# Three more clearing matmuls ahead of the first transposition

## The chip, the cores and the metric

The kernel runs on one core of a Trainium2 chip. The metric is the time of one execution on the device in microseconds (us); the median of three runs of the kernel before is 458.16 us (457.68 to 458.56). Profiles are of one execution each, and times inside them count from the first instruction.

## The reference, cut to what matters

Two layers are applied in turn, twice: a sliding-window attention (32 heads of 16, window 256) and a dense layer with a gelu, both behind a layer norm and with a residual. x is 2048 x 512 in bf16.

```python
x = A_x
x = x + _A_ref(_layernorm(x, axis=-1), A_wqkv, A_wo)
x = x + _B_ref(_layernorm(x, axis=-1), B_w1, B_b1, B_w2, B_b2)
x = x + _A_ref(_layernorm(x, axis=-1), A_wqkv, A_wo)
x = x + _B_ref(_layernorm(x, axis=-1), B_w1, B_b1, B_w2, B_b2)
```

The instructions that the change adds compute nothing of this. They multiply zeros by zeros and write zeros into PSUM, and every later user of PSUM starts its own sum.

## The kernel before, in words

The 2048 rows are cut into 16 tiles of 128 rows, and two tiles make an attention block. For each tile the layer norm takes the statistics on VectorE (bn_stats, L727; bn_aggr, L729; the epsilon, L731), the power of -1/2 on GpSimd (L734), and the normalised tile xn on VectorE (L737). TensorE then transposes xn in four matmuls of 128 columns against the identity (L36, called from tr, L757), and ScalarE or VectorE copies the result out of PSUM to xnTA (L713, L715). For each block, TensorE makes Q and K (groups of four matmuls with 256 columns, L32) and V (512 columns). ScalarE and VectorE move these out of PSUM (Q: L713 and L715; K: L824; V: L713). Then TensorE makes scores for 512 positions at a time and ScalarE takes their exponential (L903), a mask is multiplied in (L924), and E times V follows. Layers of the dense part run between these visits.

Nothing is scheduled while the program runs. Each piece of work is a node, added with `add`; a list ORDER, written out by hand, says in which order the nodes are put on their engines, TURNS which engine takes a node that has a choice, BANKS which PSUM bank it gets. `run` of the class `_List` walks that list and works out a start and an end of each node from stated durations. These times decide no order. They are used in one place, `spread`: an instruction of TensorE that would wait for several semaphores hands some of these waits to earlier matmuls that, by the planned times, start late enough. So a stated duration can move a wait from one matmul to another, and does nothing else.

The engine with the change is TensorE. Its program begins with two clear nodes (L665 to L677): VectorE sets a tile of zeros, and the two nodes multiply it by itself into PSUM banks 0 to 7, and then again into banks 0 to 4, 13 matmuls of 512 columns in all. They wait for the zeros alone. Behind them TensorE's queue holds four transpositions of tile 0, four of tile 1, 12 matmuls for Q and K of block 0, eight transpositions of tiles 2 and 3, 22 more matmuls for Q and K, and the first 16 matmuls of the scores. TensorE takes its queue in this order.

The loads go out on the queues of SyncE and ScalarE at the start: x in four pieces, and the three parts of the Q, K, V weights, then Wo, W1 and W2.

```python
for n, took in ((8, 3420.0), (5, 1300.0)):
    add("pe", clear(n), took, reads=["zero", "g0"], writes=["ps:init0", "ps:init1"], prio=-200, geo="f")
```

Of the kernel before, what the change touches and what calls it, by code (L numbers as in the profile page):

```python
# [185 lines left out]
class _List:  # L186
# [13 lines left out]
    def add(self, eng, fn, dur, reads=(), writes=(), prio=0.0, alloc=(), free=(), after=(), geo=None, table=None,  # L200
            issue=0.0, alt=(), war=(), lock=False, joins=()):

        i = len(self.nodes)
        deps = set(after)
        for r in tuple(reads) + tuple(joins):
            if r in self.lw:
                deps.add(self.lw[r])
        for w in tuple(writes) + tuple(war):
            if w in self.lw:
                deps.add(self.lw[w])  # L210
            deps.update(self.lr.get(w, ()))
        for r in reads:
            self.lr.setdefault(r, []).append(i)
        for w in writes:
            self.lw[w] = i
            self.lr[w] = []
        deps.discard(i)
        n = 0
        if eng == "pe":
            c = _Count()  # L220
            fn(c, _Anywhere())
            n = c.n
        self.nodes.append(dict(
            eng=eng, fn=fn, dur=dur, reads=list(reads), writes=list(writes), prio=prio, joins=tuple(joins),
            jdeps=frozenset(self.lw[r] for r in joins), alloc=alloc, free=tuple(free), deps=deps, geo=geo, table=table,
            issue=issue, lock=lock, alts=((eng, fn, dur),) + tuple(alt), n=n, behind=None,
            heavy=any(a[0] == "pool" and a[2] > 600.0 for a in ((eng, fn, dur),) + tuple(alt)),
        ))
        return i
# [69 lines left out]
def bass_interleave_layers__sliding_block__dense_activation_gelu__prompt_kernel(  # L299
# [72 lines left out]
    with ExitStack() as kctx:  # L372
# [294 lines left out]
        def clear(n):  # L667

            def fn(e, B):
                for b in range(n):  # L670
                    r = e.matmul(ps[:, b, :], gT[:, 0, 0:P], zero, start=True, stop=True)
                return r

            return fn

        for n, took in ((8, 3420.0), (5, 1300.0)):
            add("pe", clear(n), took, reads=["zero", "g0"], writes=["ps:init0", "ps:init1"], prio=-200, geo="f")  # L677

        def dma(fn, writes, reads=(), dur=2200.0, prio=0.0, issue=640.0, eng="sp"):
# [431 lines left out]
        for i in order:  # L1111
            nd = PL.nodes[i]
            n = 1
            if nd["eng"] == "pe":
                c = _Count()
                nd["fn"](c, B)
                n = c.n
# [32 lines left out]
```

## Time and profile before

| | |
|---|---|
| median of three runs | 458.16 us |
| lowest, highest | 457.68, 458.56 us |
| the profiled execution's own time | 460.18 us |
| its span, first to last instruction | 458.4 us |
| outside the span | 1.8 us |
| TensorE busy | 444.1 us, 97% |
| ScalarE busy | 389.7 us, 85% |
| VectorE busy | 368.5 us, 80% |
| mean granted clock of TensorE | 0.993 |

The profiled execution is 2.0 us longer than the median. A row of the timeline gives the start, the length, the engine, the line, the operation, what it writes and reads, how many instructions are merged in it, and in brackets how long the engine was idle before, and what ended that. A row of the windows gives a stretch, its length, for each engine the busy time and in brackets the number of instructions that touch it, the granted TensorE clock as a share of full speed, the DMA share and the rate. The clock's first record begins at 6.05 us; ahead of it the column prints 1.00 without a record.

### The profile page before, as it was taken

The numbers are of one execution on the slowest core, as the hardware profiler recorded it, in microseconds if no ns is written. First come the engines' busy times: TensorE is split into PE (matmuls) and PEld (weight loads), VectorE is DVE, ScalarE is ACT, GpSimd is POOL, SyncE is SP. The second block draws the span as 40 slices with busy tenths as digits, with TensorE's granted clock in tenths as the row PEclk, the third lists the DMA queues.
The fourth block names the chain that finished last, engine by engine and source line by source line (L and its number), as shares of the span: only waits on it lengthen the run. The fifth ranks groups of instructions, "written<-read, shape, count | busy, mean of one in ns | idle before, by whom it ended". The sixth has DMA issues, their size and how long they took to land.

```text
span 458.4 us, 19422 instructions
## 1 busy us (share of the span) xinstructions
PE 444.1 (97%) x8790; PEld 238.7 (52%) x8790; DVE 368.5 (80%) x749; ACT 389.7 (85%) x462; POOL 234.7 (51%) x266
## 2 busy tenths in 40 slices
PE   7999999989899999999999999999999999999997
PEld 3655655645453554645455545546464554545664
DVE  5899988999777888989889888899788888677411
ACT  2899999999789999899997999889987999792442
POOL 5377666565768266332565467754355243462400
PEclk9999999999989999999999999999999999999999
DMA  8910000001110020100120000201012002201211
GB/s 271 370 62 4 4 3 3 4 3 26 40 35 1 9 44 9 43 3 11 21 68 3 5 23 15 60 9 24 3 23 58 3 11 52 72 2 33 67 52 36
DMA packets 27839, 18.17 MB, mean 40 GB/s; under 512 B 15852, under 2 KB 27244, under 8 KB 27756
## 3 DMA queue, kind: packets, MB, share of 16 engines
q1 hardware_dynamic: 26172, 15.35, 12.8%
q8 instruction: 69, 1.13, 1.1%
q10 hardware_dynamic: 1584, 1.57, 1.0%
q14 instruction: 14, 0.11, 0.1%
HBM read 11.41 MB, written 5.51 MB: 37 GB/s over the span
## 4 chain that ended last, share of the span: by engine, by line
PE 75%; ACT 21%; DVE 1%; DMA 1%; issue 1%
PE ps L32 74%; ACT E L903 16%; ACT gT L1069 2%; ACT gT L1061 1%; PE ps L36 1%; ACT L903 1%; ACT L1061 1%; DMA X<-in_A_x_dram 1%; DVE stat L727 0%; DVE X L784 0%; DVE xn L737 0%; ACT xnTA L715 0%; DVE statmv L729 0%; DVE veps L731 0%
## 5 line engine op out<-in xcount | busy, mean ns | idle before, releaser
L903 ACT ACTIVATE E<-ps 128x1024 bf16<-128x1024 f32 x304 | 286.3, 1048 | 24.9 <-PE ps L32 24.1
L924 POOL TENSOR_TENSOR E<-E,mask 128x512 bf16<-128x512 bf16 (+1 forms) x133 | 140.3, 1070 | 91.8 <-DVE E L924 46.9
L32 PE MATMUL ps<-W_sb,gT 128*128 128x512 bf16 x448 | 120.1, 380 | 0.0
L32 PE MATMUL ps<-xnTB,W_sb 128*128 128x512 bf16 (+1 forms) x560 | 113.1, 337 | 0.0
L32 PE MATMUL ps<-xnTA,Wqkv_sb 128*128 128x256 bf16 x512 | 76.3, 279 | 1.2 <-ACT xnTA L715 0.7
L32 PEld LDWEIGHTS ps<-xnTB,W_sb 128*128 128x128 bf16 x560 | 51.6, 98 | 43.4 <-ACT E L903 3.9
L784 DVE TENSOR_TENSOR X<-X,ps 128x512 bf16<-128x512 bf16 x64 | 43.3, 681 | 33.9 <-PE ps L32 33.0
L1069 ACT ACTIVATE gT<-ps,b1T 128x512 bf16<-128x512 f32 (+1 forms) x92 | 48.5, 588 | 23.9 <-PE ps L32 23.4
L32 PE MATMUL ps<-QT,KT 32*64 32x320 bf16 (+4 forms) x2976 | 65.7, 259 | 2.9 <-ACT E L903 1.2
L734 POOL TENSOR_TENSOR rstd<-veps,mhalf 128x1 f32<-128x1 f32 x64 | 36.2, 572 | 52.2 <-DVE veps L731 50.4
L32 PEld LDWEIGHTS ps<-W_sb,gT 128*128 128x128 bf16 x448 | 39.6, 98 | 42.2 <-issue 8.4
L32 PEld LDWEIGHTS ps<-xnTA,Wqkv_sb 128*128 128x128 bf16 x512 | 47.2, 100 | 23.9 <-issue 3.1
L32 PEld LDWEIGHTS ps<-QT,KT 32*64 32x64 bf16 x2976 | 27.6, 103 | 51.1 <-ACT E L903 32.3
L924 DVE TENSOR_TENSOR E<-E,mask 128x512 bf16<-128x512 bf16 (+1 forms) x129 | 51.1, 424 | 2.5 <-ACT E L903 2.5
L32 PE MATMUL ps<-E,Va 64*17 64x128 bf16 (+3 forms) x3872 | 49.3, 230 | 3.5 <-issue 1.7
L1033 POOL TENSOR_TENSOR X<-X,b2b 128x512 bf16<-128x512 bf16 x32 | 36.6, 1153 | 30.0 <-DVE TM L994 12.4
L989 DVE STREAM_TRANSPOSE TT<-ps 128x1024 f32<-128x1024 f32 x32 | 39.9, 1248 | 13.8 <-PE ps L32 13.1
L32 PEld LDWEIGHTS ps<-E,Va 64*17 64x17 bf16 x3872 | 39.5, 85 | 19.1 <-PE ps L32 6.3
L727 DVE BATCH_NORM_STATS2 stat<-X 128x6 f32<-128x512 bf16 x64 | 43.0, 678 | 3.9 <-DMA X<-in_A_x_dram 3.4
L824 DVE TENSOR_TENSOR KT<-ps,parmask 128x1024 bf16<-128x1024 f32 x32 | 38.6, 1206 | 1.3 <-PE ps L32 1.2
L1058 DVE TENSOR_SCALAR gT<-ps,b1T 128x512 bf16<-128x512 f32 (+1 forms) x48 | 31.8, 672 | 6.9 <-PE ps L32 6.3
L32 PE MATMUL ps<-Wqkv_sb,xnTA 128*128 128x512 bf16 x128 | 36.8, 381 | 0.5 <-issue 0.5
(49 smaller groups left out, 330.0 us busy)
## 6 DMA issues: line engine op xcount, KB each, us to landing
W_sb<-in_B_w_dram SPq DMA_DIRECT2D x2, 1792.0 KB, 17.5
scr_x<-xs_ SPq DMA_DIRECT2D x104, 32.0 KB, 1.6
xnTB<-scr_x SPq DMA_DIRECT2D x26, 128.0 KB, 2.8
out_dram<-X SPq DMA_DIRECT2D x16, 128.0 KB, 1.7
Wqkv_sb<-in_A_wqkv_dram ACTq DMA_DIRECT2D x3, 512.0 KB, 7.5
X<-in_A_x_dram SPq DMA_DIRECT2D x1, 1024.0 KB, 12.2
X<-in_A_x_dram SPq DMA_DIRECT2D x2, 256.0 KB, 4.6
X<-in_A_x_dram SPq DMA_DIRECT2D x1, 512.0 KB, 8.8
```

The lines of the kernel that those rows point to most:

```text
L32: return self.e.matmul(*a, **k)
L727: add("dve", lambda e, B: e.bn_stats(stat6[:, k6, :], X[:, t, :]), 590, reads=["X%d" % t], writes=["st%d" % k6], prio=prio)
L734: add("pool", lambda e, B: e.tensor_tensor(out=rstd[:, k : k + 1], in0=veps[:, k : k + 1], in1=mhalf[:], op=ALU.pow), 535, reads=["ve%d" % ...
L784: add("dve", lambda e, B: e.tensor_tensor(out=X[:, t, :], in0=X[:, t, :], in1=ps[:, B[g][0], :], op=ALU.add), d_psum(512), reads=["X%d" % ...
L824: add("dve", lambda e, B, g=g, i=i: e.tensor_tensor(out=KT[:, kb, :, 2 * i : 2 * i + 2, :].rearrange("p a c q -> p a (c q)"), in0=ps[:, B[ ...
L903: add("act", lambda e, B, g_=g_, gi=gi: e.activation(E[:, 2 * gi : 2 * gi + 2, e0 : e0 + 512], ps[:, B[g_][0] : B[g_][0] + 2, :], AF.Exp, ...
L924: op = lambda e, B, Ew=Ew, Mw=Mw: e.tensor_tensor(out=Ew, in0=Ew, in1=Mw, op=ALU.mult)
L989: add("dve", lambda e, B: e.transpose(TT[:, s].rearrange("p a c q d -> p a (c q d)"), ps[:, B[g][0] : B[g][0] + 2, :].rearrange("p a n -> ...
L1033: add("pool", lambda e, B: e.tensor_tensor(out=X[:, t, :], in0=X[:, t, :], in1=b2b[:], op=ALU.add), 1110, reads=["X%d" % t, "b2b"], writes ...
L1058: add("dve", lambda e, B, g=g, fc=fc: e.tensor_scalar(out=gT[:, fc, 0:M], in0=ps[:, B[g][0], 0:M], scalar1=b1T[:, fc : fc + 1], scalar2=No ...
L1061: add("act", lambda e, B, fcs=fcs: e.activation(gT[:, fcs[0] : fcs[-1] + 1, 0:M], gT[:, fcs[0] : fcs[-1] + 1, 0:M], AF.Gelu_apprx_tanh, sc ...
L1069: add("act", lambda e, B, g=g, fc=fc: e.activation(gT[:, fc, 0:M], ps[:, B[g][0], 0:M], AF.Gelu_apprx_tanh, bias=b1T[:, fc : fc + 1], scal ...
```

## The change

The second of the two clear nodes clears eight banks in place of five, so that there are 16 clearing matmuls in place of 13. Its stated duration goes from 1300 to 2000 ns.

```diff
-        for n, took in ((8, 3420.0), (5, 1300.0)):
+        for n, took in ((8, 3420.0), (8, 2000.0)):
             add("pe", clear(n), took, reads=["zero", "g0"], writes=["ps:init0", "ps:init1"], prio=-200, geo="f")
```

In the built programs the instructions of VectorE, ScalarE, GpSimd and SyncE and their waits are the same. On TensorE three matmuls are added behind the 13th, and two waits move: one for a DMA goes from a score matmul to the matmul with W1 right behind it, and one for ScalarE goes from the last of four transpositions to the score matmul right behind it.

## Prediction

> **What bounds the kernel now.** First the page's busy shares and its clock row, to see which engine is full and where its clock drops.
>
> ```profile
> PE 444.1 (97%) x8790; PEld 238.7 (52%) x8790; DVE 368.5 (80%) x749; ACT 389.7 (85%) x462; POOL 234.7 (51%) x266
> ...
> PEclk9999999999989999999999999999999999999999
> ```
>
> TensorE (PE) is busy 97% of the span. The clock row's slices are 11.5 us long and hide a short drop; the windows view below shows two. Next, the chain of waits, followed from the first transpositions on.
>
> ```profile
> 8.01 0.41 PE ps L36 x4
> 8.42 0.02 issue
> 8.44 0.61 ACT xnTA L715
> 9.04 0.05 issue
> 9.09 2.42 PE ps L32 x12
> 11.51 0.85 PE ps L36 x8
> 12.37 8.78 PE ps L32 x128
> 21.14 0.02 issue
> 21.16 27.61 ACT E L903 x30
> ```
>
> From 9.09 us PE work alone sets the pace up to 21.14; then ScalarE's exponentials follow one another for 27.61 us. What PE saves before 15 us brings the first exponential (15.51 us in ScalarE's timeline) forward, and all behind it. Ahead of 9.09 the chain is the load of x and the layer norm: the clears are not on it. Third, the windows view: PE's busy time in stretches of 3.41 us, and its granted clock.
>
> ```profile
> 6.05:9.47 3.42, 1.71 (x15) 1.00 1.09 349
> 9.47:12.88 3.41, 3.41 (x23) 0.50 1.10 350
> ...
> 29.95:33.36 3.41, 2.64 (x116) 1.00 0.02 5
> 98.21:101.63 3.42, 2.71 (x172) 1.00 0.02 5
> 122.11:125.52 3.41, 1.68 (x115) 1.00 0.33 66
> 125.52:128.93 3.41, 3.41 (x65) 0.50 0.54 137
> ...
> 453.20:456.61 3.41, 2.30 (x11) 1.00 0.23 77
> ```
>
> The clock is halved twice, each time for 3.41 us, and the distances between its changes are multiples of 3.41 (12.88 to 125.52 is 33 of them). Both times the stretch just before held little PE work: 1.71 and 1.68 us. The stretches with 2.30, 2.64 and 2.71 were not followed by a drop. So in this trace the limit lies **between 1.71 and 2.30 us of busy PE in 3.41**. The clears themselves show a half clock up to 6.05: their starts lie 0.427 apart until then, later 0.216.
>
> The first drop, 9.47 to 12.88, lies on the chain: the Q and K matmuls of 256 columns start 0.213 us apart in it, and 0.109 behind it.
>
> **The change part by part.** PE's timeline at the start:
>
> ```profile
> 1.25 5.33 PE L32 MATMUL ps<-gT 128*128 128x512 bf16 x13 [1.25 <-DVE gT L665]
> 7.09 0.40 PE L36 MATMUL ps<-ident,xn 128*128 128x128 bf16 x4 [0.50 <-DVE xn L737]
> 8.01 0.40 PE L36 MATMUL ps<-ident,xn 128*128 128x128 bf16 x4 [0.52 <-DVE xn L737]
> 9.09 2.42 PE L32 MATMUL ps<-xnTA,Wqkv_sb 128*128 128x256 bf16 x12 [0.69 <-ACT xnTA L715]
> ```
>
> *The three clears by themselves.* At 0.216 each they take 0.65 us. The 13th starts at 6.21, so the 14th to 16th start at 6.42, 6.64 and 6.85, and PE can take the next at 7.07. The first transposition starts at 7.09, when VectorE's xn is there. Cost 0: the idle 0.50 covers it. If all three still ran at half clock they would take 1.28 and delay tile 0 by 0.61 (6.42 + 1.28 against 7.09); but tile 1's transposition at 8.01 and its copy at 8.44 are what the chain goes through, 0.92 behind tile 0's, so only what goes past that would cost.
>
> *What they do to the clock.* They fill the idle 0.50 in the stretch 6.05 to 9.47 and bring it from 1.71 to **2.21 us**. That lies between the limits, 0.09 from the upper one: five sixths of the way. I take the near row and hold that the clock isn't halved.
>
> *What that is worth.* At full clock the 12 matmuls from 9.09 last 12 x 0.109 = 1.31, to 10.40 (in the trace to 11.31). The transpositions of tile 2 follow (xn is there at 9.55). Tile 3's xn is ready only at 10.97 (VectorE's L737 at 9.99, 0.98 long), so its four run from 11.02 to 11.24, in the trace to 12.16: 0.92 gained. Six more matmuls take 0.65; the seventh waits for VectorE's copy of tile 3, which comes 0.24 behind the transposition and takes 0.42, so it starts at 11.95, in the trace at 13.17: **1.22 gained**. From there both run at full clock. The K copy (L824, 13.37 to 14.60) is held by VectorE's queue behind the same copy and comes forward with it. So the scores start at 13.8 in place of 15.01. No load stands in the way: the last part of Wqkv lands at 11.78 and V first uses it at 15.81. Bounds: 0 (clock still halved) to 1.22.
>
> If the 3.41 us grid lay 1.4 us earlier in another execution, the half clock would be over by 11.48, with tile 3 transposed at about 11.98 instead of 12.16, and 0.75 would be gained. I take **1.05**, between 0.75 and 1.22.
>
> [...]
>
> *The moved waits.* One goes to the next matmul, one over a transposition to the matmul behind it; nothing is between. W1 had landed at 21.20, and its first matmul is at 52.68. Bounds -0.05 to 0.05 (a short idle of PE); taken as 0.
>
> *The program's place.* Six instructions (three loads, three matmuls) come in early, so whatever is tied to a fixed place in PE's code now comes three matmuls sooner. PE stood still for 1.73 us at 125.47 with no releaser ("issue"), and 0.46 at 292.57. The matmuls around the first lie 0.01 to 0.1 apart, around the second 0.2: bounds -0.3 to 0.3 for each; taken as 0.
>
> Sum: in the profiled execution 460.18 - 1.22 = 458.96, on its own grid. That execution is 2.0 us over the median, so the absolute number is made from the median: 458.16 - 1.05 = **457.1**, a gain of 0.23%. About 0.2%, 0.92 us, is what a measurement of this kernel can tell from no change.
>
> **The rivals.**
>
> *The clock is halved anyway* (chance 0.24; 458.2, within 457.7 to 458.6). Either the limit is between 2.21 and 2.30, or what counts isn't the busy time of these rows: counted from start to start, the transpositions' 0.40 each shrinks to 0.22. For it: without the transpositions' 0.79 the stretch holds 0.92, with the clears 1.57; the other halved stretch then holds 1.42 and the lowest that isn't halved 2.02 (29.95), so by that count 1.57 is nearer to the halved ones. Against it: nothing in this trace separates the two counts. [...]
>
> *The drop comes later, on denser work* (0.09; 459.0, slower). If the grid lies 2.1 us earlier (changes at 3.95, 7.36, 10.78), 13 clears end at about 5.4 and leave 1.45 + 0.27 of 3.41 up to 7.36: halved until 10.78, which covers only matmuls that partly wait for tile 3 anyway, a loss of about 0.4. Sixteen clears add 0.65, so that stretch passes, but the next, 7.36 to 10.78, holds 0.40 for tile 1 and 1.69 from 9.09 on, 2.09 in all; if the limit is over that, 10.78 to 14.19 is halved, with the last transposition and nearly all 22 matmuls in it, a loss of about 1.3. It ends 0.9 slower. It decides where the limit lies between 2.09 and 2.30 and the grid in such a place.
>
> *The drop at 125.52 goes or comes* (0.09; half 456.4, half 459.9). The stretch with 1.68 holds the whole 1.73 stall. Brought forward by about 1 us, the stall can fall across two stretches, and neither is under the limit: the 3.41 at half clock, worth up to 1.7, goes. In executions where it was split before, it can come.
>
> **How the numbers follow.** The forecast has 0.58 (456.7 to 457.6); some two thirds of that is under 457.24, the bound. Faster: 0.38 + 0.04 = 0.42. Same: 0.20 + 0.24 + 0.05 = 0.49. Slower: 0.04 + 0.05 = 0.09. The chance of "same" is the largest since a gain of 1.05 hardly passes the bound. Range: the forecast, the clock halved anyway, and half of the later drop: 456.2 to 458.9, which leaves out less than 2 in 10.
>
> **What would show it.** In the changed kernel's profile: 16 clears that end at about 7.1 and no idle before tile 0's transposition; in the windows view a clock of 1.00 from the clears' end up to 15 us; the 12 matmuls from 9.09 in 1.5 us; the first exponential (L903) near 14.3. If the clock is halved there again, the limit or the count is wrong, and the time is that of before. If the first exponential comes early and the end doesn't, the gain is lost behind 21 us, against the chain above.

## The result, and the profile after

| | before | after |
|---|---|---|
| median | 458.31 us (19 runs) | 460.03 us (19 runs) |
| lowest, highest | 457.68, 459.41 | 458.83, 464.59 |
| profiled execution, its span | 460.18, 458.4 us | 461.06, 459.3 us |

The changed kernel is **slower**, by 0.4%: ratio 1.0044, 95% interval 1.0028 to 1.0061. The ratios given here are taken over all runs and differ a little from those of the two medians. The forecast was 457.1 (456.2 to 458.9).

The start went as forecast in the main. PE's timeline of the changed kernel, at the rows shown of before:

```profile
1.25 4.92 PE L32 MATMUL ps<-gT 128*128 128x512 bf16 x16 [1.25 <-DVE gT L665]
6.87 0.40 PE L36 MATMUL ps<-ident,xn 128*128 128x128 bf16 x4 [0.70 <-DVE xn L737]
7.79 0.40 PE L36 MATMUL ps<-ident,xn 128*128 128x128 bf16 x4 [0.52 <-DVE xn L737]
8.88 1.49 PE L32 MATMUL ps<-xnTA,Wqkv_sb 128*128 128x256 bf16 x12 [0.69 <-ACT xnTA L715]
...
11.05 2.60 PE L32 MATMUL ps<-xnTA,Wqkv_sb 128*128 128x256 bf16 x22
13.58 0.42 PE L32 MATMUL ps<-QT,KT 32*64 32x256 bf16 x16
```

The 12 matmuls take 1.49 us in place of 2.42, and ScalarE's first exponential starts at 14.08 in place of 15.51. The clears ended at 6.17, not at 7.1, since the clock's first record begins at 3.90 here and not at 6.05: the clears start 0.427 us apart up to 3.79 and 0.216 apart from 4.06 on. The grid of 3.41 us lies elsewhere in each profile (edges at 6.05 in before, 3.90 here, 5.47 in eleven, 5.92 in late). The page's clock row has no drop at all:

```profile
PEclk9999999999999999999999999999999999999999
```

So the gain is there at 15 us and gone at the end. The same instruction of ScalarE, looked up in both traces, shows where (after minus before): -1.35 us at 10.62 of the changed kernel, -2.16 at 126.94 (the drop at 125.52 is missing too), -1.17 at 281.84, +0.02 at 291.88, -0.57 at 295.69 (before's own stop, shown below, lies just ahead), +0.20 at 305.11, +0.84 at 397.50. It is lost in **a few places of about 1 us each**. One of them, in the timeline of PE's weight loads (PEld), which has all 8793 records where 73 matmul records are missing:

```profile
290.19 0.15 PEld L32 LDWEIGHTS ps<-QT,KT 32*64 32x64 bf16 x14 [0.42 <-issue]
291.56 0.10 PEld L32 LDWEIGHTS ps<-QT,KT 32*64 32x64 bf16 x2 [1.22 <-issue]
```

In before the same 16 loads come in one go, and a shorter stop lies behind them and two more:

```profile
291.36 0.16 PEld L32 LDWEIGHTS ps<-QT,KT 32*64 32x64 bf16 x16 [0.42 <-issue]
291.72 0.10 PEld L32 LDWEIGHTS ps<-W_sb,gT 128*128 128x128 bf16 x1 [0.20 <-issue]
291.73 0.10 PEld L32 LDWEIGHTS ps<-Wqkv_sb,xnTA 128*128 128x128 bf16 x1
292.57 0.31 PEld L32 LDWEIGHTS ps<-W_sb,gT 128*128 128x128 bf16 x2 [0.74 <-issue]
```

PE's weight loads stop for 1.22 us in the middle of 16 matmuls of one form, with nothing in the profile that releases them ("issue"). That such a stop falls four loads earlier than before's points at PE's own program. The page lists a DMA queue of instructions, in both kernels alike:

```profile
q8 instruction: 69, 1.13, 1.1%
```

69 transfers of 16 KB (1.13 MB / 69) for 8790 matmuls: one for about 127 matmuls, if all of them are PE's. That the stops hang on these transfers is a theory so far; the last section of the experiments has the test of it.

### The profile page after: what moved, and what is told of

Read it like the earlier page. It is cut to its first block, busy times and chain, and to the rows that moved or that the text cites. A ratio compares the mean times of both kernels' runs of the same rounds, so it can differ in the third digit from the quotient of the medians.

```text
span 459.3 us, 19357 instructions
## 1 busy us (share of the span) xinstructions
PE 432.0 (94%) x8720; PEld 236.8 (52%) x8793; DVE 368.0 (80%) x749; ACT 389.7 (85%) x462; POOL 234.9 (51%) x266
## 3 DMA queue, kind: packets, MB, share of 16 engines
q8 instruction: 69, 1.13, 1.1%
## 4 chain that ended last, share of the span: by engine, by line
PE 69%; ACT 18%; DVE 7%; issue 3%; DMA 2%; SPq 1%; POOL 0%
PE ps L32 67%; ACT E L903 13%; ACT gT L1069 2%; PE ps L36 1%; DVE stat L727 1%; SPq L750 1%; ACT gT L1061 1%; DVE X L784 1%; DVE QT L713 1%; ACT L903 1%; DVE xn L737 1%; DMA X<-in_A_x_dram 1%; DMA xnTB<-scr_x 1%; DMA scr_x<-xs_ 1%; DVE xs_ L746 1%
## 5 line engine op out<-in xcount | busy, mean ns | idle before, releaser
L32 PE MATMUL ps<-W_sb,gT 128*128 128x512 bf16 x404 | 108.9, 380 | 4.5 <-issue 3.5
L32 PE MATMUL ps<-xnTA,Wqkv_sb 128*128 128x256 bf16 x512 | 74.0, 273 | 2.2 <-issue 0.8
L32 PEld LDWEIGHTS ps<-xnTA,Wqkv_sb 128*128 128x128 bf16 x512 | 46.2, 98 | 24.5 <-issue 4.1
L32 PE MATMUL ps<-Wqkv_sb,xnTA 128*128 128x512 bf16 x113 | 33.0, 380 | 1.9 <-issue 1.3
```

Of the source, the lines that this page charges most:

```text
L32: return self.e.matmul(*a, **k)
```

## The experiments

Three theories. **A**: PE's program comes in blocks of about 128 matmuls (8790 for 69 transfers are 127 for one), and three more matmuls ahead move the edge of each block by three; where PE reaches an edge before the next block is there, it stops. **B**: the early start itself is lost again in later waits, or the added matmuls cost by what they do at the start. **C**: the two moved waits. Each run is compared with the kernel before on the same chip; "measured" gives the two medians in us, then the ratio and its 95% interval.

### Three short matmuls, and the fill without them

tiny3: before, and three short matmuls behind the 13 clears (with 9 and 36 in later runs).

```diff
+            for i in range(3):
+                h, r = i % 2, i // 2 % 4
+                x = e.matmul(ps[32 * r : 32 * r + VW, 5 + h, 0:64], gT[HK * h : HK * h + HK, 0, 0:VW],
+                             gT[HK * h : HK * h + HK, 0, 0:64], start=True, stop=True)
```

> The 13 clears of before, and behind them three matmuls of 64 columns with 17 weights, some 0.01 us each, in place of three clears. TensorE's program is as long as in the changed kernel, with the same two moved waits, but the idle time before the first transposition is not filled. Theory A (what costs is the place of the program: its code comes in blocks of about 128 matmuls, and three more matmuls ahead move every block's edge by three matmuls, so that PE waits for code at other places): as slow as the changed kernel or slower, 460 to 461.5 us. Theory B (what costs is the early start: without the half clock the work comes 1.2 us early and loses it again in waits further on): 458.3, as before. Theory C (the two moved waits cost): 460 to 461, as A; the run with the waits put back tells these two apart.

Measured 458.42 against 457.14: 1.0029 (1.0017 to 1.0042). Three matmuls that fill nothing cost 1.3 us. A's direction holds, its 460 doesn't, as this chip's before is 1.2 us under the earlier one. B's second part stays possible.

late: before, with a wider memset ahead of the clears; PE's program is unchanged.

```diff
-        add("dve", lambda e, B: e.memset(zero, 0.0), 120, writes=["zero", "g0"], prio=-300)
+        add("dve", lambda e, B: e.memset(gT[:, 0:5, :], 0.0), 120, writes=["zero", "g0", "g1", "g2", "g3", "g4"], prio=-300)
```

> The program of before with not one instruction of TensorE changed; the zero tile's memset on VectorE is five times as wide, so that the 13 clears start about 1.1 us later and end near the first transposition. The idle time is filled without moving the code. Theory A: the early start is kept and nothing is lost behind it, 457.2 us (0.7 to 1.4 under before). Theory B: as slow as the changed kernel, 460. Theory C: 457.2.

Measured 457.44 against 457.14: 1.0009 (0.9994 to 1.0024). The idle time is filled and the clock full:

```profile
2.32 4.74 PE L32 MATMUL ps<-gT 128*128 128x512 bf16 x13 [2.32 <-DVE gT L665]
6.90 0.39 PE L36 MATMUL ps<-ident,xn 128*128 128x128 bf16 x4
7.54 0.40 PE L36 MATMUL ps<-ident,xn 128*128 128x128 bf16 x4 [0.26 <-DVE xn L737]
8.63 1.49 PE L32 MATMUL ps<-xnTA,Wqkv_sb 128*128 128x256 bf16 x12 [0.69 <-ACT xnTA L715]
```

So an early start does not end slower (against B), and also **it brings nothing** over the median of before: all three theories had missed that. The likely reason lies in the executions of before that were timed beside the experiments: of 98, 80 had a mean granted clock of 0.999 or 1.000 and 18 one of 0.995 or 0.996, which is one half-clock stretch (3.41 x 0.5 / 458 = 0.004). By batch the medians of the 18 lie 1.0 to 2.0 us above those of the 80. The profile that the forecast was read from, 0.993 with two such stretches and 460.18 us, is the rare case. (The mean counts only what the trace has records of, so 18 is what shows, not a bound.)

### The waits, and a whole block

waits: the changed kernel with the planner's count of code three matmuls lower, which puts both waits back.

```diff
-        code, edge, loaded = 2.0, self.CODE[0], 0.0
+        code, edge, loaded = 2.0 - 3 * self.CODE[2], self.CODE[0], 0.0
```

> The changed kernel with its 16 clears, with the two moved waits put back to the matmuls where they stand in the kernel before (the planner's count of code starts three matmuls lower; nothing else differs). Theory A: 460.0 us, no change from the changed kernel. Theory B: 460.0. Theory C: 457.2.

Measured 458.39 against 457.14: 1.0028 (1.0011 to 1.0045). It has 16 clears and no moved wait, and costs what tiny3 costs with both. C falls.

block: 128 matmuls more than before. The second clear node clears 128 columns of five banks, and 128 short matmuls (`small`, the loop of tiny3) follow.

```diff
-        for n, took in ((8, 3420.0), (5, 1300.0)):
...
+        def second(e, B):
+            for b in range(5):
+                e.matmul(ps[:, b, 0:128], gT[:, 0, 0:P], zero[:, 0:128], start=True, stop=True)
+            return small(e, 128)
+
+        for fn, took in ((clear(8), 3420.0), (second, 1300.0)):
```

> Eight clears of 512 columns, five of 128, and 128 matmuls of 64 columns with 17 weights: 128 matmuls more than before, one whole block of TensorE's code, so that the edges of the blocks lie at the same matmuls as before, with about the fill of the changed kernel; banks 0 to 4 are cleared a second time in part only. The waits stand as before. Theory A: 457 to 458.3 us, since the edges are back where they were. Theory B: 460, since the start is early. Theory C: 457 to 458.3.

Measured 457.02 against 457.14: 0.9994 (0.9984 to 1.0004). **Three more matmuls cost 1.2 us, 128 more cost nothing.** The page has one transfer more:

```profile
q8 instruction: 70, 1.15, 1.0%
```

block3: the block run and three more.

> The block run's kernel (eight clears of 512 columns, five of 128, 128 short matmuls) with three short matmuls more: one block and three. The waits stand as before. Theory A: as the run with three short matmuls, 1.3 us over the kernel before, 458.4. Theory B: as the block run, 457.0, since 0.03 us more at the start is nothing.

Measured 458.95 against 457.86: 1.0027 (1.0005 to 1.0049). With block it fits a period of 128 matmuls, tried at this one length. B's second half falls: 128 added matmuls cost nothing at the start, and three behind them cost 1.1 us.

### More and fewer matmuls

From here on the waits are put back in the same way, so that only the place of the program differs.

tiny36: the loop of tiny3 with 36 short matmuls.

> The 13 clears of before and 36 matmuls of 64 columns behind them, some 0.01 us each; the waits stand where they stand before. Theory A (the blocks of code): TensorE's program lies 36 matmuls further on against its blocks. Laid over the times of the block run, with 3.4 us for each block's load (the constant in the planner's CODE), blocks with many short score and E times V matmuls would now be run through faster than the next one comes, in sum 9 to 15 us: 465 to 473 us. Theory B (the cost of the earlier runs comes from what the added matmuls do at the start): 457 to 459, since they take under 1 us.

Measured 477.05 against 457.86: 1.0440 (1.0405 to 1.0475), 19 us for 36 matmuls that together take under 1 us. A foretold 7 to 15, with 3.4 us for each block's load. No run shows that term: the transfers of q8 take 1.2 us each in the mean in before (1.1% of 16 engines' 458.4 us, over 69), and 53 of 54 stops of PE end 2.16 to 2.96 us after one begins (last section of the experiments).

tiny9: the same loop with nine.

> The same with nine short matmuls; the waits stand where they stand before. Theory A: the same sum is lowest for six to eleven matmuls, 0.0 us, against 1.7 for none and 1.4 for three (measured: three cost 1.3 more than none, so the sum is no better than 1.5 us): 455.5 to 458.5 us. Theory B: the more matmuls, the more cost, 458.4 or over.

Measured 463.35 against 457.86: 1.0126 (1.0104 to 1.0149). A's direction, but its number was wrong: the sum had the minimum here. That sum took the edges from the planner's constants and put one at the 2507th matmul behind the clears in before; before's trace has the stop at the 2496th. It also rests on the 3.4 us for each load, so its sizes are the author's estimate alone; measured are 1.3, 5.5 and 19 us for 3, 9 and 36 more.

full9: 16 clears and six short matmuls.

> The 16 clears of the changed kernel and six short matmuls, nine more in all than before; the waits stand where they stand before. Theory A: as the run with nine short matmuls, less what the filled idle time brings, which the late run puts at nothing in most executions: 455 to 458.5, and under the changed kernel. Theory B: as the changed kernel, 458.4 or over.

Measured 463.32 against 457.86: 1.0121 (1.0100 to 1.0142). It is over the changed kernel and not under it as A had said, by the same wrong sum. It has tiny9's time (463.35) with three clears more and three short matmuls fewer, so here again the fill changes nothing.

eleven and nine: 11 and 9 clears, `(8, 3420.0), (3, 1300.0)` and `(1, 1300.0)`.

> 11 clears in place of 13, two matmuls fewer than before; the waits stand where they stand before. Theory A (the blocks of code): the edges move the other way, by two matmuls. Three more cost 1.2 us, nine 5.5, so the cost is flat or falls this way: 456.5 to 457.8 with 457.5 before on the same chip. Theory B (any three matmuls more at the start cost): two fewer gain, 456.5 or under. The idle time before the first transposition grows by 0.4 us; where the clock is halved for that, 1.2 us more.

Measured 458.12 against 457.78: 1.0021 (0.9999 to 1.0042), not told from no change.

> Nine clears, four matmuls fewer than before; the waits stand where they stand before. Theory A: the edges move by four matmuls the other way; flat, or slower where a new block's edge comes to lie badly: within 1 us of before. The fill is 0.9 us less, so by the limit of about 1.75 us of busy PE in 3.41 the clock should be halved at the start in more of the executions, each 1.2 us slower.

Measured 459.20 against 457.78: 1.0038 (1.0021 to 1.0054). The smaller fill shows in the clock: ten of nine's 12 executions have a granted clock of 0.996 or less, seven of eleven's 12, and seven of 29 of before in that batch. In eleven the five others have a median of 457.27 and these seven 458.66. In nine the two others took 458.97 and 459.22, no less than the ten (median 459.21), so it isn't shown that nine's 1.4 us come from the clock. Eleven's windows view shows the half clock behind a stretch of 1.48 us:

```profile
5.47:8.89 3.42, 1.48 (x13) 1.00 1.10 353
8.89:12.30 3.41, 3.41 (x22) 0.50 1.10 348
```

narrow: 13 clears of 64 columns each, PE's code unchanged; the clears do not cover the banks.

```diff
-                    r = e.matmul(ps[:, b, :], gT[:, 0, 0:P], zero, start=True, stop=True)
+                    r = e.matmul(ps[:, b, 0:64], gT[:, 0, 0:P], zero[:, 0:64], start=True, stop=True)
```

> 13 clears of 64 columns in place of 512: TensorE's code and waits are those of before, and only the fill is gone (banks are cleared in their first 64 columns). PE then works 0.7 us of its first 5.8. If the fill is what keeps the first Q and K matmuls at full clock, these 34 matmuls and eight transpositions run at half clock until a stretch is over half full, and the time is 1.2 to 2.5 us over before. If the fill is worth nothing, as before.

Measured 459.66 against 457.78: 1.0047 (1.0027 to 1.0066), 1.9 us. Without the fill of the 13 clears the kernel is that much slower; late, whose fill reaches to the first transposition, gained nothing over it. The spacing of its 12 matmuls, 0.21 us, is that of the half clock (0.213 in before's halved stretch, 0.109 behind it), though the trace has no clock record:

```profile
9.10 2.74 PE L32 MATMUL ps<-xnTA,Wqkv_sb 128*128 128x256 bf16 x12 [0.69 <-ACT xnTA L715]
```

That the clock comes back once a stretch is over half full is shown only within wide bounds: it came back behind 2.65 us of busy PE (0.49 to 3.90 in the changed kernel), and did not behind 1.39 (up to 2.64 in before, whose clears go on 0.427 apart to 5.92).

fourteen: 14 clears, as a candidate to beat both.

> 14 clears, one matmul more than before; the waits stand where they stand before. Theory A: three more cost 1.2 us, so one costs 0.0 to 0.6, less what 0.2 us more fill saves in the executions whose clock is halved at the start (about one in six so far, 1.2 us each, so 0.2 at most): from 0.2 under the kernel before to 0.6 over it. It would beat both kernels only at the lower end.

Measured 457.82 against 457.71: 1.0012 (0.9990 to 1.0033). With one more clear its profile shows no drop at the start, with 1.96 us in the stretch that had 1.71 in before:

```profile
6.14:9.56 3.42, 1.96 (x16) 1.00 1.09 347
9.56:12.97 3.41, 3.19 (x34) 1.00 1.10 350
```

No run beat the kernel before beyond its interval; block, at 0.9994, came nearest.

### The stops move with the program

Where PE's weight loads stop for over 0.4 us without a stop at the same load in all kernels, at three places, by the number of the load counted from the first transposition, which is the same piece of work everywhere:

| matmuls more than before | one stop | a second | a third |
|---|---|---|---|
| -4 (nine) | 2500 | none | none |
| -2 (eleven) | 2498 | none | none |
| 0 (before, late, block, narrow) | 2496 | 5943 | none |
| +1 (fourteen) | none | 5942 | none |
| +3 (changed kernel) | 2493 | 5939 | 6194 |
| +3 (tiny3) | none | 5939 | 6194 |
| +3 (waits, block3) | none | 5940 | none |
| +9 (tiny9) | none | 5934 | 6189 |

The 16 score loads of the fences above are cut in tiny9 again, five loads earlier than in the changed kernel:

```profile
291.92 0.13 PEld L32 LDWEIGHTS ps<-QT,KT 32*64 32x64 bf16 x9 [0.42 <-issue]
293.24 0.12 PEld L32 LDWEIGHTS ps<-QT,KT 32*64 32x64 bf16 x7 [1.18 <-issue]
```

Counted from the program's beginning (the clears added), these stops stay where they are: 2496 + 13 and 2493 + 16 are both 2509, and so are nine's 2500 + 9 and eleven's 2498 + 11. (5939 + 16 is one less than 5943 + 13; with the two waits put back it is 5940.)

The packet records of the traces tie the stops to the instruction queue. In the 14 profiles there are 54 stops of the weight loads of over 0.43 us that nothing in the profile releases. They last 0.45 to 2.17 us, yet 53 of them end 2.16 to 2.96 us after a transfer of q8 begins (the other 3.75); these transfers come 6.3 us apart in the mean. The stop shown above that ends at 291.56 has its transfer at 289.41, the only one of q8 between 289.40 and 292. The DMA view of 289.40 to 289.42 has its one packet:

```profile
q8 instruction: 1, 0.02, 295.3%
```

An edge doesn't always give a stop: of the four kernels with three matmuls more, only the changed kernel's profile has the one at 2493. Nor does a stop simply cost what it lasts. PE stands for 2.1 us without a releaser in tiny3's profile and for 1.9 in late's. Exponential by exponential, tiny3 is 1.24 us ahead of late at 122.88, where it has no stop, and of this 0.10 is left at 262.51. It loses 0.41 us at 280.10, 0.91 at 289.86 and 0.68 at 303.00, right behind its stops at 5684, 5939 and 6194, regains 0.59 at 293.67, and ends 1.2 behind.

## Why the prediction was wrong, point by point

- **The three clears by themselves, cost 0**: right in the changed kernel's profile, where they ended 0.70 us before the first transposition. That the clock rose 2.15 us earlier than in before was luck. In full9's profile the clears' weight loads lie 0.43 us apart up to 6.77, the spacing of the half clock (0.427 up to 5.92 in before), and the first transposition starts at 7.66 with xn written at 7.00; yet the 12 matmuls start at 9.23 against 9.09 in before, so only 0.14 us gets through, as the prediction argued.
- **The limit of the clock**: the fill was held to be enough, and it is, in that the changed kernel's profile has no drop. But the bounds 1.71 and 2.30 were wide: late has a stretch of 1.78 us (121.98 to 125.39) and the changed kernel one of 2.10 (7.31 to 10.73) that no drop follows. In these profiles the limit lies between 1.71 (before, halved behind it) and 1.78 us of busy PE in 3.41. The rival's count without transpositions, with all other matmuls taken alike, does not fit: without them fourteen's stretch from 6.14 holds 1.17 us and no drop follows, while before's from 122.11 holds 1.42 and one does. A count that also takes the small matmuls of 122.11 for less is not told apart.
- **What that is worth, 1.05 us**: wrong for the median. In the profiled executions the exponentials come 1.43 us early, of which 0.22 is an earlier x (the first transposition at 6.87 instead of 7.09); that leaves 1.21, as summed. But the sum took one execution's half clock for every execution's. With 13 clears 18 of 98 show any, and late, which has the fill and no other change in PE's program, gains nothing. That the grid lies elsewhere in each execution was weighed only as a smaller gain, not as no gain.
- **The program's place, "-0.3 to 0.3, taken as 0"**: this is the step that failed. It named the two stops and that what is tied to a place in PE's code comes three matmuls sooner, and then bounded each by the spacing of the matmuls around it. Even there the bound was passed: the weight loads' 0.74 at 292.57 became 1.22 at 291.56. And it left out the edges at which before did not stop at all: in the changed kernel's profile 0.84 us at 280.56 and 0.90 at 303.87. Tiny3 measures the sum at 1.3 us without the fill and waits at 1.25 with it.
- **The moved waits, 0**: right, by waits against tiny3.
- **The rivals**: "the clock is halved anyway", "the drop comes later" and "the drop at 125.52" all looked to the clock. The changed kernel shows a half-clock stretch in 2 of its 19 executions, so none of them makes its median. The drop at 125.52 did go between the two profiles, in the way described: the stall lies across the edge of two stretches at 123.37, and the later has 2.04 us of busy PE. None had the cause.

One loss of the changed kernel's profile stays open: 0.68 us at 396.02, where a matmul waits for xnTB's transfer (L754). It was not tried by itself; tiny3's profile, with the same place of the program, does not have it, and fourteen's, with another, has one of 0.82 at the same matmul, so it does not follow the program's place alone.

## What to carry to other kernels

When instructions are added to an engine whose program is long and dense, count where all later code comes to lie, not only what the new instructions take: here three matmuls of nothing cost 0.28% and 128 cost none. Look for stops without a releaser ("issue") and for the instruction queue's transfers in the page, and keep the place (pad to a whole block, 128 matmuls here, or lengthen what is there) before judging an edit. And before an edit is worked out from a drop of the clock in one profile, see in how many executions that drop is there at all.

## What the runs showed of the hardware that was not expected

PE stops at places that stay fixed in its program (2509 matmuls from its beginning in six profiles) and so move against the work when matmuls are added: 36 short matmuls ahead of a tuned order cost 19 us of 458, in stops of up to 2.2 us, and 128 cost nothing. Measured are the page's 69 instruction transfers of 16 KB, 70 with 128 matmuls more; the changed kernel's stops at 5684, 5939 and 6194, 255 loads (2 x 127.5) from one to the next; and 53 of 54 stops, 0.45 to 2.17 us long, that end 2.16 to 2.96 us after such a transfer begins. That the code comes in blocks of about 127 matmuls with their weight loads, at whose end PE waits for the next, is the author's reading of these numbers; no view shows a block itself. The clock was halved for 3.41 us after a stretch of 3.41 with 1.71 us of busy PE (before), and not after one with 1.78 (late). The profile's clock column prints 1.00 where it has no record, also over matmuls that run at half clock (narrow, up to about 12 us).
